# Decode attention beside a gated unit on one core: products with V by two chunks in head-group order, starting three slots later

## The chip, the cores and the metric

The kernel runs on one core of one Trainium2 chip. The metric is the device time of one execution in microseconds (us). For the kernel before, three runs were timed; their median is 198.92 us. One execution was also recorded by the hardware profiler. Engines go by the names of the profile: PE is TensorE (PEld its weight loads), DVE is VectorE, ACT is ScalarE, POOL is GpSimd, SP is SyncE, whose queue (SPq) issues nearly all transfers here.

## What is computed

One decoding step for 8 sequences: attention over the last 2048 entries of a cache, multiplied by a gate from a small feed-forward unit, added to the input. The reference, cut to what matters (B = 8, D = 512, 32 query heads on 8 K/V heads, head size 128, F = 1792; all in bf16):

```
xn = layernorm(x)                                # 8 rows of 512
W  = 2048                                        # the window: the last 2048 of 8192 cache rows
q  = (xn @ wq)                                   # 32 heads of 128 per row
scores = q . k_cache[:, :, -W:, :] * 128 ** -0.5 # 4 query heads share one K/V head
o  = softmax(scores) @ v_cache[:, :, -W:, :]
s  = o @ wo
h  = sigmoid(xn @ w_gate) * (xn @ w_up)
out = x + s * silu(h @ w_down)
```

The windows of K and of V are 33.6 MB each. With the weights, 81.01 MB are read from HBM in one execution.

## The kernel before, in words

**Tiles.** K comes in 8 tiles of 4 MB (four sequences, all 8 heads, a quarter of the window each; line 125), V in 16 tiles of 2 MB (`load_v`, line 137: one sequence, a head group of 4 K/V heads, the whole window in 64 chunks of 32 rows). The sequences fall into two halves, hb = 0 and 1, of four sequences. K tiles 0 to 3 and V tiles 0 to 7 belong to half 0. wq, the K tiles, the gate and up weights, the down weights and wo share a ring of three buffers (KRING); V has a ring of four (VRING). A load can start when the tile three (or four) before it in its ring has been read for the last time.

**Slots.** The order of the work is written out by hand: a loop over slots t (line 651) calls the stages, and each engine runs its instructions in the order in which the loop emits them. Slots 0 to 63 each turn an eighth of a K tile in place on DVE (`k_turn`, line 433, L441). Four slots later `qk` (line 443, L456) multiplies that eighth with the queries on PE; after 8 slots a tile's scores are complete, and a maximum is taken on DVE (L470). EXP_AT is 36 and 68: there `soft_exp` (line 474) makes the exponentials of a half on ACT (L484). One slot later `soft_turn` turns them on DVE (L504), two slots later `soft_spread` spreads them over partitions on PE (L517), copied out by ACT (L525). `soft_mask` (line 531, L539) multiplies them by a mask for each of four heads on DVE, so that one matmul can serve four heads; there is one buffer of these masked exponentials, pT_sb, for both head groups of a half. `soft_den` (line 549) makes the reciprocals of the denominators.

**Products with V.** `pv` (line 580, L595) handles a quarter of a V tile in one slot. PV_AT is 49 for half 0 and 83 for half 1: V tiles 0 to 7 take slots 49 to 80, then two slots are free, and tiles 8 to 15 take slots 83 to 114. The masks are at slots 47 and 48, and at 81 and 82; the denominators at 48 and 82. V tile i is sequence i // 2, head group i % 2. Tiles 0 to 7 are multiplied four chunks at a time (16 matmuls of 128x512 for a tile, two side by side in the array), tiles 8 to 15 two chunks at a time (32 matmuls of 128x256, four side by side). ACT copies the sums out (L606); in the next tile's first slot `pv_sum` (line 609) adds the parts with small f32 matmuls (L616), and DVE scales them (L625).

**Loads.** `issue_loads` (line 198) emits the loads in one fixed order, sorted by the slot of first use (line 184): wq, K0 to K6, V0, V1, K7, V2 to V13, gate and up, V14, V15, down, and wo in eight pieces. All of them are issued by SP in this order, each after a wait for its buffer; a load whose buffer is not free holds back those behind it.

**End.** After the last V tile `o_rows` gathers the heads (L639), `unit_out` makes the gate (L358, with the down weights), and 64 matmuls multiply with wo (L702) as its pieces arrive; two DVE instructions and two small stores end the kernel.

Of the kernel before, what the change touches and what calls it, by code (L numbers as in the profile page):

```python
# [10 lines left out]
def kernel(  # L11
# [13 lines left out]
    nc = tc.nc  # L25
    P = 128
    B, _, D = A_x.shape
    _, Hkv, Sk, Dh = A_k_cache.shape
    Hq = A_wq.shape[1] // Dh
    rep = Hq // Hkv  # L30
# [11 lines left out]
    GL = 4  # L42
    NG = Hkv // GL
    PP = P // GL
    CH = W // PP
    NQ = P // 32
    NJ = 4
    CC = CH // NJ
    NT = B * NG
    NSLOT = NT * NJ  # L50


    HB = B // NQ
# [7 lines left out]
    VSET = NT // HB  # L61
    QK_LAG = 4
    EXP_AT = [SET * (hb + 1) + QK_LAG for hb in range(HB)]
    PV_LAG = 13
    PV_AT = [EXP_AT[0] + PV_LAG]
    for hb in range(1, HB):
        PV_AT.append(max(EXP_AT[hb] + 5, PV_AT[hb - 1] + VSET * NJ + 2))


    NA = Dh // 64  # L70
    CB = CH // 2
    PV_WIDE = VSET
    KRING = 3
    VRING = 4
    NCOL = 2
# [2 lines left out]
    bf16 = mybir.dt.bfloat16  # L78
    f32 = mybir.dt.float32
    AF = mybir.ActivationFunctionType  # L80
    ALU = mybir.AluOpType
    AX = mybir.AxisListType
# [2 lines left out]

    consts = ctx.enter_context(tc.tile_pool(name="consts", bufs=1))
    work = ctx.enter_context(tc.tile_pool(name="work", bufs=1))
    small = ctx.enter_context(tc.tile_pool(name="small", bufs=2))
    kring = ctx.enter_context(tc.tile_pool(name="kring", bufs=KRING))
    vring = ctx.enter_context(tc.tile_pool(name="vring", bufs=VRING))  # L90
# [4 lines left out]
    psum_a = ctx.enter_context(  # L95
        tc.tile_pool(name="psum_a", bufs=3, space=bass.MemoryType.PSUM)
    )
# [25 lines left out]
    v_tiles = {}  # L123

    def load_k(i):
# [8 lines left out]
        )  # L134
        k_tiles[i] = t

    def load_v(i):
        b, gg = divmod(i, NG)
        t = v_tile([P, CH, Dh], "v_sb")
        load(  # L140
            t[:].rearrange("p c d -> p (c d)"),
            A_v_cache[b, GL * gg : GL * (gg + 1), win0:Sk, :].rearrange(
                "j (p c) d -> p j (c d)", c=CH
            ),
        )
        v_tiles[i] = t
# [18 lines left out]
    def load_wo():  # L165
# [19 lines left out]
        (kind, i)  # L185
        for _, kind, i in sorted(
            [(KTS * i, 0, i) for i in range(NKT)]
            + [(NJ * (i % VSET) + PV_AT[i // VSET], 1, i) for i in range(NT)]
        )
    ]  # L190
    loads[-2:-2] = [(2, 0)]
# [6 lines left out]
    def issue_loads():  # L198
# [16 lines left out]
    ident = consts.tile([P, P], bf16, name="ident")  # L215
# [19 lines left out]
        out=rstd[:], in_=mv[:, 1:2], func=AF.Sqrt, bias=eps_t[:], scale=1.0  # L235
# [4 lines left out]
        out=xn_bf[:],  # L240
# [7 lines left out]
    for kt in range(KT):  # L248
        nc.tensor.transpose(
            out=xnT_ps[:, kt, :], in_=xn_bf[:B, kt::KT], identity=ident[:B, :B]  # L250
        )
    x2_ps = psum1.tile([NCOL * 32, DC], f32, name="x2_ps", tag="misc")
    for c in range(NCOL):
        nc.tensor.matmul(
            x2_ps[32 * c : 32 * (c + 1), :],
            lhsT=ident[:B, :32],
            rhs=x_bf[:, DC * c : DC * (c + 1)],
            start=True,
            stop=True,
# [17 lines left out]
        out=PermF[:], in_=ident[:].rearrange("m (h q r) -> m q h r", q=NQ, r=rep)  # L277
# [4 lines left out]
        out=Hm[:],  # L282
        in_=ident[:].rearrange("p (a gl) -> p gl a", gl=GL),
        axis=AX.X,
        op=ALU.add,
# [4 lines left out]
    for j in range(GL):  # L290
        for gg in range(NG):
            g = NG * gg + j // 2
            nc.vector.tensor_copy(
                out=spread[:, gg, j % 2, :, j], in_=ident[:, 32 * g : 32 * g + PP]
            )

    Sel = {}
    for w in (32, 64):
        rows_of = small.tile([P, w], f32, name=f"rows_of{w}")
        nc.vector.tensor_reduce(  # L300
            out=rows_of[:],
            in_=ident[:].rearrange("p (a m) -> p m a", m=w),
            axis=AX.X,
            op=ALU.add,
        )
        Sel[w] = consts.tile([P, w // 16, GL, rep], f32, name=f"Sel{w}")
        by_row = rows_of[:].rearrange("p (h g c r) -> p h c g r", g=GL, c=2, r=rep)
        for c in range(w // 16):
            nc.vector.tensor_copy(out=Sel[w][:, c], in_=by_row[:, c // 2, c % 2])

    NE = P // Hq
    pick = consts.tile([32 * NG, NE, P], bf16, name="pick")
# [1 line left out]
    for gg in range(NG):  # L314
        rows = slice(32 * gg, 32 * (gg + 1))
        cols = slice(NE * GL * rep * gg, NE * GL * rep * (gg + 1))
        for e in range(NE):
            nc.vector.tensor_copy(
                out=pick[rows, e, cols].rearrange("p (h d) -> p h d", d=NE)[:, :, e],
                in_=ident[rows, 32 * gg : 32 * gg + GL * rep],  # L320
# [104 lines left out]
    pT_of = {}  # L425
    den_of = {}
    rden_of = {}
    acc_tiles = {}
# [101 lines left out]

    def soft_mask(hb, gg):

        if gg == 0:
            pT_of[hb] = work.tile(
                [P, NG, NQ * CB, GL, 2 * rep], bf16, name="pT_sb", tag="pT_sb"
            )
        pc = pc_of[hb][:, gg].rearrange("p q (c e) r -> p (q c) (e r)", e=2)
        for gl in range(GL):
            nc.vector.tensor_scalar(  # L539
                out=pT_of[hb][:, gg, :, gl, :],  # L540
                in0=pc,
                scalar1=Hm[:, gl : gl + 1],
                scalar2=None,
                op0=ALU.mult,
            )
# [34 lines left out]
    def pv(t):  # L580


        i, j = divmod(t, NJ)
        b, gg = divmod(i, NG)
        n_ch = 4 if i < PV_WIDE else 2
        w = 16 * n_ch
        if j == 0:
            acc_tiles[i] = psum_a.tile([P, n_ch * Dh], f32, name="acc_ps", tag="acc_ps")
        pT = pT_of[b // NQ][:, gg, CB * (b % NQ) : CB * (b % NQ + 1)].rearrange(
            "p c g n -> p (c g n)"  # L590
        )
        for n in range(CC // n_ch):
            c = n % (P // w)
            ch = CC * j + n_ch * n
            nc.tensor.matmul(  # L595
                acc_tiles[i][w * c : w * (c + 1), :],
                lhsT=pT[:, 16 * ch : 16 * ch + w],
                rhs=v_tiles[i][:, ch : ch + n_ch, :].rearrange("p c d -> p (c d)"),
                start=(j == 0 and n < P // w),
                stop=(j == NJ - 1 and n >= CC // n_ch - P // w),  # L600
                tile_position=(0, w * c),
                skip_group_check=True,
            )
        if j == NJ - 1:
            acc_sb = small.tile([P, n_ch * Dh], f32, name="acc_sb")
            nc.scalar.copy(out=acc_sb[:], in_=acc_tiles.pop(i)[:])  # L606
            acc_sbs[i] = acc_sb

    def pv_sum(i):
        b, gg = divmod(i, NG)  # L610
        n_ch = 4 if i < PV_WIDE else 2
        acc_sb = acc_sbs.pop(i)
        rows = slice(32 * gg, 32 * gg + GW)
        o_ps = psum1.tile([32 * NG, Dh], f32, name="o_ps", tag="misc")
        for c in range(n_ch):
            nc.tensor.matmul(  # L616
                o_ps[rows, :],
                lhsT=Sel[16 * n_ch][:, c].rearrange("p g r -> p (g r)"),
                rhs=acc_sb[:, Dh * c : Dh * (c + 1)],
                start=(c == 0),  # L620
                stop=(c == n_ch - 1),
                tile_position=(0, 32 * gg),
                skip_group_check=True,
            )
        nc.vector.tensor_scalar(  # L625
            out=o_sb[rows, b, :],
            in0=o_ps[rows, :],
            scalar1=rden_of[b // NQ][rows, b % NQ : b % NQ + 1],
            scalar2=None,
            op0=ALU.mult,  # L630
        )
# [16 lines left out]
        )  # L648

    KSLOT = NKT * KTS  # L650
    for t in range(PV_AT[-1] + VSET * NJ):
        u = -1
        for hb, at in enumerate(PV_AT):
            if 0 <= t - at < VSET * NJ:
                u = t - at + VSET * NJ * hb
        if QK_LAG + KTS <= t <= KSLOT + QK_LAG and (t - QK_LAG) % KTS == 0:
            soft_max_part((t - QK_LAG) // KTS - 1)
        for hb in range(HB):
            if t == EXP_AT[hb]:
                soft_exp(hb)  # L660
            for gg in range(NG):
                if t == PV_AT[hb] - NG + gg:
                    soft_mask(hb, gg)
        if t < KSLOT:
            k_turn(t)
        if t == 1:
            q_out(1, q_tiles[1], (0,))
        for hb in range(HB):
            if t == EXP_AT[hb] + 1:
                soft_turn(hb)  # L670
        if QK_LAG <= t < KSLOT + QK_LAG:
            qk(t - QK_LAG)
        if u >= NJ and u % NJ == 0:
            pv_sum(u // NJ - 1)
        if u >= 0:
            pv(u)
        for hb in range(HB):
            if t == EXP_AT[hb] + 2:
                soft_spread(hb)
            if t == PV_AT[hb] - 1:  # L680
                soft_den(hb)
        if t >= QK_LAG and (t - QK_LAG) % KTS == KTS - 1:
            released.add((0, (t - QK_LAG) // KTS))
        if u >= 0 and u % NJ == NJ - 1:
            released.add((1, u // NJ))
        issue_loads()
        if u == NSLOT - 2 * NJ - 1:
            unit_in(wgu_sb[0])
            unit_in(wgu_sb[1])
            released.add((2, 0))  # L690
            issue_loads()
        if u == NSLOT - 2 * NJ:
            unit_mid()
# [6 lines left out]
    for k in range(KW):  # L700
        for c in range(NCOL):
            nc.tensor.matmul(  # L702
                a_ps[32 * c : 32 * (c + 1), :],
                lhsT=o2_sb[:, k, :],
                rhs=wo_parts[k][:, DC * c : DC * (c + 1)],
                start=(k == 0),
                stop=(k == KW - 1),
# [8 lines left out]
    for c in range(NCOL):  # L716
        queues[c].dma_start(
            out=out.flatten_outer_dims()[:, DC * c : DC * (c + 1)],
# [32 lines left out]
```

## Time and profile before

| what | value |
|---|---|
| three timed runs | 197.73, 198.92, 199.18 us; median 198.92 |
| the profiled execution's own time | 199.89 us |
| its span, first to last instruction | 198.1 us |
| DVE busy | 110.8 us (56%), of it 73.9 in the K turns |
| PE busy | 99.1 us (50%); granted clock 0.854 on average |
| ACT busy | 29.1 us (15%) |
| transfers | 81.16 MB, 410 GB/s on average over the span |

The span is 1.8 us shorter than the execution's own time; what lies around it is the launch and the end. The profiled execution took 0.97 us longer than the median of the timed runs, so that a saving read from the trace is subtracted from the median, not from the profiled time. In the timeline of the trace a line gives the start and the duration of an instruction or of a merged group, its engine, line, operation and tile, and in square brackets how long the engine had been idle before it and what released it.

### The profile page before, as it was taken

What the parts mean: (1) busy time and instruction counts of PE and PEld (TensorE: products, weight loads), DVE (VectorE), ACT (ScalarE), POOL (GpSimd) and SP (SyncE); (2) the same over time, 40 slices, a digit from 0 to 9 for tenths busy, and PEclk for the clock granted to TensorE, in tenths of its full rate; (3) what the DMA queues carried; (4) which work ended last, traced back from release to release, by engine and by line L of the source; (5) the groups of instructions that cost most, each with busy time, mean ns of one, the idle gap of its engine ahead of it and who ended that gap; (6) DMA issues with size and microseconds to landing.
All of it is one profiled execution on the core that took longest, in us unless ns stands there. A gap on an engine that the chain in (4) does not pass through costs nothing.

```text
span 198.1 us, 2316 instructions
## 1 busy us (share of the span) xinstructions
PE 99.1 (50%) x950; PEld 43.9 (22%) x950; DVE 110.8 (56%) x182; ACT 29.1 (15%) x69; POOL 1.6 (1%) x8
## 2 busy tenths in 40 slices
PE   0133024434333039314986984888277633545693
PEld 0010001101011012001222331334045421223381
DVE  4706499999899969997995832501711100030301
ACT  3006050000000264000110115151101003000000
POOL 3000000000000000000000000000000000000000
PEclk9999999999999999855897999589958995555569
DMA  7999999999999999899999999999998999999990
GB/s 260 443 443 443 424 419 424 430 424 420 430 463 430 450 443 423 377 440 450 430 417 427 424 443 424 427 409 384 424 430 334 425 426 433 442 427 416 415 377 20
DMA packets 5242, 81.16 MB, mean 410 GB/s; under 512 B 600, under 2 KB 880, under 8 KB 1392
## 3 DMA queue, kind: packets, MB, share of 16 engines
q1 hardware_dynamic: 5200, 81.01, 96.4%
q8 instruction: 7, 0.11, 0.2%
q10 hardware_dynamic: 32, 0.01, 0.0%
q14 instruction: 3, 0.02, 0.0%
HBM read 81.01 MB, written 0.01 MB: 409 GB/s over the span
## 4 chain that ended last, share of the span: by engine, by line
DMA 53%; PE 20%; DVE 18%; ACT 6%; issue 2%; SPq 1%; ACTq 0%; DVEq 0%
DMA k_sb<-in_A_k_cache_dram 20%; DMA wd_sb<-in_B_w_down_dram 15%; DMA v_sb<-in_A_v_cache_dram 13%; DVE k_sb L441 12%; PE acc_ps L595 8%; PE o_ps L616 5%; DMA wo_sb<-in_A_wo_dram 5%; PE s_ps L456 3%; ACT p_bf L484 3%; PE pT_ps L517 2%; ACT acc_sb L606 2%; DVE pT_sb L539 2%; DVE pt_bf L504 1%; DVE mx L470 1%; SPq L108 1%
## 5 line engine op out<-in xcount | busy, mean ns | idle before, releaser
L441 DVE STREAM_TRANSPOSE k_sb<-k_sb 128x1024 f32<-128x1024 f32 x64 | 73.9, 1211 | 4.2 <-DMA k_sb<-in_A_k_cache_dram 4.1
L456 PE MATMUL s_ps<-k_sb,qz_sb 128*32 128x512 bf16 x256 | 29.3, 552 | 47.1 <-DVE k_sb L441 41.3
L595 PE MATMUL acc_ps<-v_sb,pT_sb 128*32 128x256 bf16 (+1 forms) x384 | 34.5, 371 | 9.2 <-DMA v_sb<-in_A_v_cache_dram 9.2
L625 DVE TENSOR_SCALAR o_sb<-o_ps,rden 16x128 bf16<-16x128 f32 x16 | 5.5, 341 | 49.3 <-PE o_ps L616 49.3
L456 PEld LDWEIGHTS <-qz_sb 128*32 128x32 bf16 x256 | 8.4, 114 | 70.7 <-issue 53.6
L616 PE MATMUL o_ps<-acc_sb,Sel 128*16 128x128 f32 x96 | 16.6, 321 | 10.5 <-ACT acc_sb L606 10.2
L606 ACT COPY acc_sb<-acc_ps 128x512 f32<-128x512 f32 (+1 forms) x16 | 7.7, 480 | 77.6 <-PE acc_ps L595 77.6
L595 PEld LDWEIGHTS <-pT_sb 128*32 128x32 bf16 (+1 forms) x384 | 14.4, 112 | 21.1 <-DMA v_sb<-in_A_v_cache_dram 9.0
L616 PEld LDWEIGHTS o_ps<-acc_sb,Sel 128*16 128x16 f32 x96 | 9.3, 109 | 18.0 <-ACT acc_sb L606 15.4
L517 PE MATMUL pT_ps<-pt_bf,spread 128*128 128x512 bf16 x16 | 6.7, 562 | 2.2 <-DVE pt_bf L504 2.0
L504 DVE STREAM_TRANSPOSE pt_bf<-p_bf 128x512 bf16<-128x512 bf16 x8 | 5.0, 680 | 4.8 <-ACT p_bf L484 4.8
L539 DVE TENSOR_SCALAR pT_sb<-pc_bf,Hm 128x1024 bf16<-128x1024 bf16 x16 | 6.5, 475 | 1.6 <-PE acc_ps L595 1.6
L470 DVE TENSOR_REDUCE mx<-s_ps 128x1 f32<-128x512 f32 x8 | 5.3, 667 | 3.6 <-PE s_ps L456 3.6
L382 PE MATMUL q_ps<-wq_sb,xnT_sb 128*32 128x512 bf16 x32 | 3.6, 630 | 7.3 <-DMA wq_sb<-in_A_wq_dram 7.3
L484 ACT ACT_TABLE_LOAD x1 | 1.3, 1283 | 39.7 <-DVE nm L478 39.7
L332 PE MATMUL d_ps<-wgu_sb,xnT_sb 128*32 128x448 bf16 x32 | 3.4, 573 | 5.7 <-DMA wgu_sb<-in_B_w_gate_dram 3.2
L484 ACT ACTIVATE p_bf<-s_ps,nm 128x512 bf16<-128x512 f32 x8 | 5.4, 686 | 4.0 <-DVE nm L478 4.0
L413 ACT COPY qz_sb<-qT_sb 32x32 bf16<-32x32 bf16 x20 | 4.8, 241 | 7.7 <-DVE qT_sb L401 7.5
L525 ACT CAST pc_bf<-pT_ps 128x512 bf16<-128x512 f32 x8 | 4.5, 587 | 8.9 <-PE pT_ps L517 6.3
L702 PE MATMUL a_ps<-wo_sb,o_sb 128*32 128x256 bf16 x64 | 5.2, 312 | 0.1
L568 PE MATMUL den_ps<-ones,dh 128*16 128x1 f32 x32 | 1.4, 166 | 6.9 <-DVE dh L555 6.4
L401 DVE STREAM_TRANSPOSE qT_sb<-q_sb 128x512 bf16<-128x512 bf16 x2 | 1.4, 690 | 6.3 <-ACT q_sb L396 6.3
(59 smaller groups left out, 42.2 us busy)
## 6 DMA issues: line engine op xcount, KB each, us to landing
k_sb<-in_A_k_cache_dram SPq DMA_DIRECT2D x8, 4096.0 KB, 21.9
v_sb<-in_A_v_cache_dram SPq DMA_DIRECT2D x16, 2048.0 KB, 17.9
wq_sb<-in_A_wq_dram SPq DMA_DIRECT2D x1, 4096.0 KB, 12.1
wo_sb<-in_A_wo_dram SPq DMA_DIRECT2D x2, 1024.0 KB
wgu_sb<-in_B_w_gate_dram SPq DMA_DIRECT2D x1, 1792.0 KB
wgu_sb<-in_B_w_up_dram SPq DMA_DIRECT2D x1, 1792.0 KB, 18.3
wd_sb<-in_B_w_down_dram SPq DMA_DIRECT2D x1, 1792.0 KB, 28.9
wo_sb<-in_A_wo_dram SPq DMA_DIRECT2D x3, 512.0 KB, 25.6
```

Of the source, the lines that this page charges most:

```text
L441: nc.vector.transpose(out=kw, in_=kw)
L456: nc.tensor.matmul(s_tiles[i][32 * g : 32 * (g + 1), :], lhsT=qz_sb[:, hb, h, 2 * a + e, :], rhs=kT[:, :, a, h, :, e], start=(n == 0), sto ...
L470: nc.vector.reduce_max(out=mx_of[hb][:, kq : kq + 1], in_=s_tiles[i][:], axis=AX.X)
L484: nc.scalar.activation(out=p_bf[:, :, kq], in_=s_tiles.pop(NK * hb + kq)[:].rearrange("p (o c j) -> p c j o", o=2, j=NC), func=AF.Exp, bia ...
L504: nc.vector.transpose(out=pt[:, w * n : w * (n + 1)], in_=p_bf[:, w * n : w * (n + 1)])
L517: nc.tensor.matmul(pT_ps[:], lhsT=spread[:, gg, y].rearrange("p k g -> p (k g)"), rhs=pt[:, c, y, :], start=(y == 0), stop=(y == 1), skip_ ...
L539: nc.vector.tensor_scalar(out=pT_of[hb][:, gg, :, gl, :], in0=pc, scalar1=Hm[:, gl : gl + 1], scalar2=None, op0=ALU.mult,)
L595: nc.tensor.matmul(acc_tiles[i][w * c : w * (c + 1), :], lhsT=pT[:, 16 * ch : 16 * ch + w], rhs=v_tiles[i][:, ch : ch + n_ch, :].rearrange ...
L606: nc.scalar.copy(out=acc_sb[:], in_=acc_tiles.pop(i)[:])
L616: nc.tensor.matmul(o_ps[rows, :], lhsT=Sel[16 * n_ch][:, c].rearrange("p g r -> p (g r)"), rhs=acc_sb[:, Dh * c : Dh * (c + 1)], start=(c ...
L625: nc.vector.tensor_scalar(out=o_sb[rows, b, :], in0=o_ps[rows, :], scalar1=rden_of[b // NQ][rows, b % NQ : b % NQ + 1], scalar2=None, op0= ...
L702: nc.tensor.matmul(a_ps[32 * c : 32 * (c + 1), :], lhsT=o2_sb[:, k, :], rhs=wo_parts[k][:, DC * c : DC * (c + 1)], start=(k == 0), stop=(k ...
```

## The change: order of V, chunk size, start slot, buffers and places of the softmax stages

1. V tiles are ordered by head group inside a half: tile i of a half is head group i // 4, sequence i % 4 (before, head group i % 2, sequence i // 2). The load order of tile numbers stays as it was.
2. All V tiles are multiplied by two chunks (before, tiles 0 to 7 by four). One selection matrix Sel is left of two.
3. V starts at slot 52 and runs without a gap to slot 115 (before, 49 to 80 and 83 to 114).
4. pT_sb becomes one buffer per half and head group, from a pool of two; each is half as large as the single one before.
5. The turn of the exponentials comes 3 slots after the exponentials (before 1), the spread 4 slots after (before 2), the denominators 5 slots after (before at slots 48 and 82, now 41 and 73). The masks are at slots 45 and 46 for half 0, and at 74 and 84 for half 1.

```diff
-    PV_LAG = 13
-    PV_AT = [EXP_AT[0] + PV_LAG]
-    for hb in range(1, HB):
-        PV_AT.append(max(EXP_AT[hb] + 5, PV_AT[hb - 1] + VSET * NJ + 2))
+    TURN_LAG = 3
+    SPREAD_LAG = 4
+    V_LAG = 49
+    PV_LAG = 52
+    MASK_AT = {}
+    for gg in range(NG):
+        MASK_AT[0, gg] = EXP_AT[0] + 9 + gg
+        MASK_AT[1, gg] = max(EXP_AT[1] + 6, PV_LAG + NJ * NQ * (gg + 1))
...
-    PV_WIDE = VSET
+    NCH = 2
...
+    work2 = ctx.enter_context(tc.tile_pool(name="work2", bufs=2))
...
+    def v_of(i):
+        hb, n = divmod(i, VSET)
+        gg, q = divmod(n, NQ)
+        return NQ * hb + q, gg
+
     def load_v(i):
-        b, gg = divmod(i, NG)
+        b, gg = v_of(i)
...
-            + [(NJ * (i % VSET) + PV_AT[i // VSET], 1, i) for i in range(NT)]
+            + [(NJ * i + V_LAG, 1, i) for i in range(NT)]
...
-        if gg == 0:
-            pT_of[hb] = work.tile(
-                [P, NG, NQ * CB, GL, 2 * rep], bf16, name="pT_sb", tag="pT_sb"
-            )
+        pT_of[hb, gg] = work2.tile([P, NQ * CB, GL, 2 * rep], bf16, name="pT_sb")
...
-        b, gg = divmod(i, NG)
-        n_ch = 4 if i < PV_WIDE else 2
-        w = 16 * n_ch
+        b, gg = v_of(i)
+        w = GL * rep * NCH
...
-    for t in range(PV_AT[-1] + VSET * NJ):
-        u = -1
-        for hb, at in enumerate(PV_AT):
-            if 0 <= t - at < VSET * NJ:
-                u = t - at + VSET * NJ * hb
+    for t in range(PV_LAG + NSLOT):
+        u = t - PV_LAG
...
-                if t == PV_AT[hb] - NG + gg:
+                if t == MASK_AT[hb, gg]:
                     soft_mask(hb, gg)
...
-            if t == EXP_AT[hb] + 1:
+            if t == EXP_AT[hb] + TURN_LAG:
                 soft_turn(hb)
...
-            if t == EXP_AT[hb] + 2:
+            if t == EXP_AT[hb] + SPREAD_LAG:
                 soft_spread(hb)
-            if t == PV_AT[hb] - 1:
+            if t == EXP_AT[hb] + 5:
                 soft_den(hb)
```

More of the change, by code (lines that the diff above doesn't have):

```diff
@@ L295 @@
             )
[L297 to L304, printed above, removed]
-        )
[L306 to L309, printed above, removed]
+    w = NCH * GL * rep
+    rows_of = small.tile([P, w], f32, name="rows_of")
+    nc.vector.tensor_reduce(
+        out=rows_of[:],
+        in_=ident[:].rearrange("p (a m) -> p m a", m=w),
+        axis=AX.X,
+        op=ALU.add,
+    )
+    Sel = consts.tile([P, NCH, GL, rep], f32, name="Sel")
+    nc.vector.tensor_copy(
+        out=Sel[:], in_=rows_of[:].rearrange("p (g c r) -> p c g r", g=GL, c=NCH)
+    )
     NE = P // Hq
@@ L531, in soft_mask @@
     def soft_mask(hb, gg):
-        if gg == 0:
-            pT_of[hb] = work.tile(
-                [P, NG, NQ * CB, GL, 2 * rep], bf16, name="pT_sb", tag="pT_sb"
-            )
+        pT_of[hb, gg] = work2.tile([P, NQ * CB, GL, 2 * rep], bf16, name="pT_sb")
         pc = pc_of[hb][:, gg].rearrange("p q (c e) r -> p (q c) (e r)", e=2)
@@ L539, in soft_mask @@
             nc.vector.tensor_scalar(
-                out=pT_of[hb][:, gg, :, gl, :],
+                out=pT_of[hb, gg][:, :, gl, :],
                 in0=pc,
@@ L583, in pv @@
         i, j = divmod(t, NJ)
-        b, gg = divmod(i, NG)
-        n_ch = 4 if i < PV_WIDE else 2
-        w = 16 * n_ch
+        b, gg = v_of(i)
+        w = GL * rep * NCH
         if j == 0:
[L588 to L592, printed above, removed]
+            acc_tiles[i] = psum_a.tile([P, NCH * Dh], f32, name="acc_ps", tag="acc_ps")
+        q = b % NQ
+        pT = pT_of[b // NQ, gg][:, CB * q : CB * (q + 1)].rearrange("p c g n -> p (c g n)")
+        for n in range(CC // NCH):
             c = n % (P // w)
-            ch = CC * j + n_ch * n
+            ch = CC * j + NCH * n
             nc.tensor.matmul(
                 acc_tiles[i][w * c : w * (c + 1), :],
-                lhsT=pT[:, 16 * ch : 16 * ch + w],
-                rhs=v_tiles[i][:, ch : ch + n_ch, :].rearrange("p c d -> p (c d)"),
+                lhsT=pT[:, GL * rep * ch : GL * rep * ch + w],
+                rhs=v_tiles[i][:, ch : ch + NCH, :].rearrange("p c d -> p (c d)"),
                 start=(j == 0 and n < P // w),
-                stop=(j == NJ - 1 and n >= CC // n_ch - P // w),
+                stop=(j == NJ - 1 and n >= CC // NCH - P // w),
                 tile_position=(0, w * c),
@@ L604, in pv @@
         if j == NJ - 1:
-            acc_sb = small.tile([P, n_ch * Dh], f32, name="acc_sb")
+            acc_sb = small.tile([P, NCH * Dh], f32, name="acc_sb")
             nc.scalar.copy(out=acc_sb[:], in_=acc_tiles.pop(i)[:])
@@ L609, in pv_sum @@
     def pv_sum(i):
-        b, gg = divmod(i, NG)
-        n_ch = 4 if i < PV_WIDE else 2
+        b, gg = v_of(i)
         acc_sb = acc_sbs.pop(i)
@@ L614, in pv_sum @@
         o_ps = psum1.tile([32 * NG, Dh], f32, name="o_ps", tag="misc")
-        for c in range(n_ch):
+        for c in range(NCH):
             nc.tensor.matmul(
                 o_ps[rows, :],
-                lhsT=Sel[16 * n_ch][:, c].rearrange("p g r -> p (g r)"),
+                lhsT=Sel[:, c].rearrange("p g r -> p (g r)"),
                 rhs=acc_sb[:, Dh * c : Dh * (c + 1)],
                 start=(c == 0),
-                stop=(c == n_ch - 1),
+                stop=(c == NCH - 1),
                 tile_position=(0, 32 * gg),
```

## The prediction

> **What bounds the kernel now.** I read the page's slices first, then the chain, then windows by stage, then the timeline of SP's issues and of PE. Slices and chain:
>
> ```profile
> DMA  7999999999999999899999999999998999999990
> GB/s 260 443 443 443 424 419 424 430 424 420 430 463 430 450 443 423 377 440 450 430 417 427 424 443 424 427 409 384 424 430 334 425 426 433 442 427 416 415 377 20
> ...
> q1 hardware_dynamic: 5200, 81.01, 96.4%
> ...
> DMA 53%; PE 20%; DVE 18%; ACT 6%; issue 2%; SPq 1%; ACTq 0%; DVEq 0%
> ```
>
> The transfers are the bound: 16 engines busy for 96.4% of the span, no compute engine above 56%. The bytes stay the same, so a gain can only come from slices in which the transfers ran below their rate; slices 27 (384) and 30 (334) stand out in the second half. The windows (engines' busy time, PE clock, DMA share, GB/s) enclose them:
>
> ```profile
> 20.00:60.00 40.00, 13.28 (x112) 4.14 (x113) 36.78 (x38) 2.90 (x12) 0.00 (x0) 1.00 1.00 432
> ...
> 110.00:132.00 22.00, 17.11 (x118) 6.45 (x116) 9.21 (x15) 6.59 (x15) 0.00 (x0) 0.84 1.01 430
> 132.00:141.00 9.00, 6.03 (x52) 3.03 (x48) 2.13 (x6) 1.76 (x3) 0.00 (x0) 1.00 0.95 381
> 141.00:148.00 7.00, 4.12 (x56) 2.72 (x56) 2.86 (x10) 0.00 (x0) 0.00 (x0) 0.69 1.01 433
> 148.00:160.00 12.00, 7.77 (x149) 5.12 (x148) 1.70 (x5) 1.86 (x5) 0.00 (x0) 0.90 0.97 393
> 160.00:184.00 24.00, 11.13 (x140) 5.75 (x141) 2.34 (x5) 2.94 (x5) 0.00 (x0) 0.59 1.00 427
> ```
>
> Two troughs, 132 to 141 and 148 to 160, each beside a stretch at 430 to 433. SP's issues show why:
>
> ```profile
> 120.97 0.54 SPq L108 DMA_DIRECT2D v_sb<-in_A_v_cache_dram  x1
> 132.27 0.54 SPq L108 DMA_DIRECT2D v_sb<-in_A_v_cache_dram  x1
> 135.85 0.54 SPq L108 DMA_DIRECT2D v_sb<-in_A_v_cache_dram  x1
> 139.48 0.54 SPq L108 DMA_DIRECT2D v_sb<-in_A_v_cache_dram  x1
> 148.22 0.53 SPq L108 DMA_DIRECT2D v_sb<-in_A_v_cache_dram  x1
> ```
>
> These are V8 to V12. A V tile (2.10 MB) takes 4.9 us at 432 GB/s, and V2 landed at 106.3 (PE waits for it until then), so V7 lands near 130.7 and V8 near 135.6: when V9 is issued at 132.27, V8 alone is in flight. The queue refills until 139.48, then 8.7 us pass without an issue. A load waits for the tile four before it to be read, so the products are late. The timeline names the two delays:
>
> ```profile
> 106.31 1.07 PE L595 MATMUL acc_ps<-v_sb,pT_sb 128*64 128x512 bf16 x4 [1.69 <-DMA v_sb<-in_A_v_cache_dram]
> 123.92 2.49 DVE L504 STREAM_TRANSPOSE pt_bf<-p_bf 128x512 bf16<-128x512 bf16 x4 [2.86 <-ACT p_bf L484]
> 137.52 1.92 PE L595 MATMUL acc_ps<-v_sb,pT_sb 128*64 128x512 bf16 x16
> 139.56 3.26 DVE L539 TENSOR_SCALAR pT_sb<-pc_bf,Hm 128x1024 bf16<-128x1024 bf16 x8 [1.58 <-PE acc_ps L595]
> 157.26 1.06 PE L595 MATMUL acc_ps<-v_sb,pT_sb 128*32 128x256 bf16 x32 [1.01 <-DMA v_sb<-in_A_v_cache_dram]
> 180.44 1.90 PE L595 MATMUL acc_ps<-v_sb,pT_sb 128*32 128x256 bf16 x32 [1.45 <-DMA v_sb<-in_A_v_cache_dram]
> ```
>
> Half 1's softmax (120 to 131) lies between products; then its masks wait for the last product of half 0, which still reads the one buffer, and with the denominators they cost 139.5 to 144.6 before the next product. From 157.26 on PE waits for V again.
>
> **The change part by part.**
>
> *Chunks.* A wide tile takes 16 matmuls in 1.92 us, a narrow one 32 in 1.06, both at a granted clock of 1.00 (1.90 at a low clock, 180.44). For eight tiles PE gains 8 x 0.86 = 6.9 us. The copy falls from 0.59 to 0.37 us, the small f32 matmuls from 8 in 1.05 to 4 in 0.61. None of this is on the path while transfers bind: it only brings releases forward, by up to 1.5 us a tile.
>
> *Selection matrices.* One reduction and five copies fewer on DVE, some 0.8 of the 1.3 us between 6.8 and 8.1; DVE then idles 6.3 us for the queries. Zero.
>
> *Turn and spread of half 0, two slots later.* DVE idled 1.94 us at 72.4 for the exponentials; two more K turns (2 x 1.16) fill it. The spread still starts with the turn's end. Denominators at slot 41 put 8 + 8 tiny matmuls (0.35 + 0.37 us) and their DVE round trip behind the spread on PE: up to 1.5 us of DVE waiting near 78, against about 1 us that leaves slot 48. K4's last product, which frees K7's buffer, may come 0.6 us later than 79.5; K6, V0 and V1 are queued then until about 92. Cover 12 us, so zero; without the cover it would be 0.6.
>
> *V three slots later.* V0's first product stood behind DVE's denominators until 92.94. In slot 52 it needs K turn 48; with masks (2 x 1.63) and maxima in between I count that turn's end at about 91.6. V4's issue, which waits for V0's last product (K turn 51), comes near 96 instead of 97.54. K7, V2 and V3 are queued until 111, so three slots (3.5 us) cost nothing even if this count is off.
>
> *Half 1.* V2 and V3 are still read on landing (106.3 and 111.2), now in slots 60 to 67, in which K7's scores end too. So exponentials start near 113.5 and not at 121.1. V4 lands at 116, and its four slots 68 to 71 need nothing of half 1. The turn (2.5) ends near 119.5; the spread is emitted behind V5's first products (V5 lands 120.9) and takes 3.1 us (128.09 to 131.2 now); V5 is read by about 125.5. Then V9 is issued near 125.5 (132.27 now), V10 near 127.5 (135.85), V11 near 132 (139.48).
>
> *Masks and buffers.* Head group 0 of half 1 is masked in slot 74, near 125 to 127, in a buffer last read by V3; V8 needs it at 135.6. Head group 1 waits at slot 84 for V7's last product (read near 132) and takes 1.63 us; queued behind it on DVE is only the scaling of V7's result, whose readers wait for nothing near. V12 needs that mask near 155. So the stall of 139.5 to 144.6 goes, and V12's issue moves from 148.2 to near 137. What is late next is V's landing itself, every 4.9 us.
>
> *Transfers.* Count, size and order stay. With two to three tiles always queued, both troughs fill at the rate of 20 to 60 us: 9.00 x (1 - 381/432) = 1.06 and 12.00 x (1 - 393/432) = 1.08, together 2.15 us. A second way: V2 to V12 is ten tiles in 157.26 - 106.31 = 50.95 us, against 10 x 4.9 = 49.0 (2.0 less) or, at 432 GB/s to the byte, 48.5 (2.4 less). I take 2.15 and keep 1.6 and 2.6 as ends. SP issues the same instructions, and POOL is not touched.
>
> [...]
>
> *The end.* Down, wo and the last products are chained to V15's landing (180.44) and move with it. One cost is unknown, PE's clock: 28 of 32 matmuls of L358 take 3.17 us at the end and L702 5.30 for 64, at a mean clock of 0.73. From 32 products in 1.06 and 1.90 us, a clock that stayed low would stretch these 8.5 us by at most about a tenth, 0.8 us, part of it still under wo's landing; a higher clock gains nothing, since wo's last piece lands at 194.6, 0.3 us before the last matmul starts to end. I take 0, the case that the trace shows, and keep +0.8.
>
> Sum against the profiled execution: 199.89 - 2.15 = 197.74. The median of the timed runs is 198.92, so 198.92 - 2.15 = 196.77: I predict 196.8, 1.1% less.
>
> **The rivals.**
>
> *Only one trough goes.* If the spread of half 1 holds PE so long that V9's issue slips past 130.7, where V8 alone is in flight, the first trough stays and only the one after the masks (1.08) fills: 197.8. For it: the spread still sits between V5's products. Against: 5 us of margin.
>
> *The troughs are not hunger.* If the rate dips there for another cause, as in slice 16 (377, with more than 10 us queued), nothing changes: 198.9. Against: 433 in 141 to 148, between the two, with V10 and V11 queued.
>
> *The end takes it back.* A low clock throughout the end gives 196.8 + 0.8 = 197.6. [...]
>
> *Slower: the new order of V lowers the rate.* Consecutive V tiles were the two head halves of one sequence; now they come from different sequences. If HBM served that worse, 33.6 MB of V (77.7 us at 432) would pay: a fall of 2.8% eats the gain, and one of 5.5% (408) costs 4.3 us and ends at 201.1. It decides from there on. Against: a K tile spans four sequences in one load and moves at 432 as well.
>
> **How the numbers follow.** Both troughs filled: 0.66, with its own range 196.3 to 197.5 (2.6 gained, to 1.6 gained with little of the end's cost). One trough or the end's cost: 0.17. No hunger: 0.08. Slower order: 0.09. About 1% is what a measurement of this kernel can tell from no change, so the border is 196.93; three quarters of the first case lie beyond it. Faster by over 1%: 0.50. Within 1%: 0.16 + 0.17 + 0.08 = 0.41. Slower: 0.09. The range 195.8 to 198.6 holds the first two cases, with the spread of the three timed runs (1.45 us) on the lower side, and leaves out the slower order and most of no hunger, some 0.17.
>
> **What would show it.** Right: windows after 110 us at 427 to 433 without a trough; V9's issue near 125, V12's near 137; masks of half 1 without 139.5's stall; V15's landing near 178; the last matmuls 2 us earlier. Wrong: a window under 400 with two V tiles queued (no hunger), an issue gap above 7 us after 120 (a new wait), V tiles more than 5.0 us apart with the queue full (the order), or a longer way from V15's landing to the end than the 14.5 us of now (the clock).

## The result and the profile after

| | before | changed |
|---|---|---|
| executions timed together | 22 | 22 |
| median | 199.25 us | 197.93 us |
| lowest to highest | 197.73 to 201.13 | 197.65 to 198.33 |
| profiled execution | 199.89 (span 198.1) | 198.09 (span 196.3) |

The ratio of changed to before is 0.9946, with a 95% interval of 0.9923 to 0.9968: a gain of 0.54%, half of the 1.1% forecast. (It leaves out executions over 1.5% above the fastest of the same kernel, so that it lies nearer to 1 than the medians' ratio.) Two things are to be explained: why the gain is half of the forecast, and why the kernel before spreads over 3.4 us and the changed one over 0.7.

The profiled execution itself went nearly as forecast. The page of the changed kernel, slices, rate and chain:

```profile
DMA  6999999999999999999999999999999999999990
GB/s 235 447 441 434 441 429 441 427 434 424 434 427 427 427 427 434 417 424 451 441 414 431 427 427 427 429 431 431 427 431 427 434 430 435 424 426 423 422 363 19
...
DMA 59%; DVE 27%; PE 9%; issue 1%; SPq 1%; ACT 0%; ACTq 0%; DVEq 0%
```

Its windows, with the columns of the prediction's windows:

```profile
110.00:132.00 22.00, 14.35 (x230) 7.81 (x222) 9.58 (x22) 6.78 (x17) 0.00 (x0) 0.84 1.01 431
132.00:141.00 9.00, 3.08 (x52) 1.75 (x52) 2.35 (x6) 0.74 (x2) 0.00 (x0) 0.80 1.00 426
141.00:148.00 7.00, 4.55 (x69) 2.38 (x62) 0.34 (x1) 0.74 (x2) 0.00 (x0) 0.50 1.02 438
148.00:160.00 12.00, 6.86 (x76) 3.40 (x76) 1.02 (x3) 0.74 (x2) 0.00 (x0) 0.50 1.00 426
```

Both troughs are gone: 426 where 381 and 393 stood. PE's clock was no better: 0.84 from 110 to 132 as before, and 0.50 from 141 to 160. The products merely had more time in hand. SP's issues of V9 to V12, and the lines of DVE and PE around half 1's softmax:

```profile
127.63 0.54 SPq L113 DMA_DIRECT2D v_sb<-in_A_v_cache_dram  x1
129.60 0.54 SPq L113 DMA_DIRECT2D v_sb<-in_A_v_cache_dram  x1
132.11 0.54 SPq L113 DMA_DIRECT2D v_sb<-in_A_v_cache_dram  x1
136.96 0.54 SPq L113 DMA_DIRECT2D v_sb<-in_A_v_cache_dram  x1
...
126.36 0.17 DVE L583 RECIPROCAL rden<-den_ps 16x4 f32<-16x4 f32 x1 [4.93 <-PE den_ps L574]
...
127.20 1.68 DVE L545 TENSOR_SCALAR pT_sb<-pc_bf,Hm 128x1024 bf16<-128x1024 bf16 x4
132.19 1.67 DVE L545 TENSOR_SCALAR pT_sb<-pc_bf,Hm 128x1024 bf16<-128x1024 bf16 x4 [1.11 <-PE acc_ps L599]
...
135.85 1.06 PE L599 MATMUL acc_ps<-v_sb,pT_sb 128*32 128x256 bf16 x32 [2.65 <-DMA v_sb<-in_A_v_cache_dram]
```

From V8 (135.85) on the first products of every tile wait for V's landing and for nothing else (eight waits, at most 2.6 us). V15 lands at 178.37 (forecast: near 178; before: 180.44).

### The profile page after: what moved, and what is told of

Read it like the earlier page. It is cut to its first block, busy times and chain, and to the rows that moved or that the text cites. A ratio compares the mean times of both kernels' runs of the same rounds, so it can differ in the third digit from the quotient of the medians.

```text
span 196.3 us, 2503 instructions
## 1 busy us (share of the span) xinstructions
PE 90.5 (46%) x1046; PEld 43.9 (22%) x1046; DVE 109.9 (56%) x176; ACT 27.4 (14%) x69; POOL 1.6 (1%) x8
## 4 chain that ended last, share of the span: by engine, by line
DMA 59%; DVE 27%; PE 9%; issue 1%; SPq 1%; ACT 0%; ACTq 0%; DVEq 0%
DVE k_sb L450 22%; DMA k_sb<-in_A_k_cache_dram 20%; DMA v_sb<-in_A_v_cache_dram 15%; DMA wgu_sb<-in_B_w_up_dram 13%; DMA wo_sb<-in_A_wo_dram 12%; PE pT_ps L526 3%; PE acc_ps L599 3%; PE s_ps L465 2%; DVE pT_sb L545 2%; DVE mx L479 1%; DVE pt_bf L513 1%; PE a_ps L702 1%; SPq L113 1%; PE den_ps L574 1%; PE o_ps L619 0%
## 5 line engine op out<-in xcount | busy, mean ns | idle before, releaser
L465 PE MATMUL s_ps<-k_sb,qz_sb 128*32 128x512 bf16 x256 | 33.3, 585 | 56.5 <-DVE k_sb L450 50.7
L599 PE MATMUL acc_ps<-v_sb,pT_sb 128*32 128x256 bf16 x512 | 31.4, 367 | 17.4 <-DMA v_sb<-in_A_v_cache_dram 17.4
L465 PEld LDWEIGHTS <-qz_sb 128*32 128x32 bf16 x256 | 10.3, 121 | 73.8 <-issue 53.2
L599 PEld LDWEIGHTS <-pT_sb 128*32 128x32 bf16 x512 | 17.9, 121 | 28.9 <-DMA v_sb<-in_A_v_cache_dram 21.3
L610 ACT COPY acc_sb<-acc_ps 128x256 f32<-128x256 f32 x16 | 6.0, 373 | 81.1 <-PE acc_ps L599 81.1
L619 PE MATMUL o_ps<-acc_sb,Sel 128*16 128x128 f32 x64 | 14.1, 362 | 6.9 <-ACT acc_sb L610 6.9
L619 PEld LDWEIGHTS o_ps<-acc_sb,Sel 128*16 128x16 f32 x64 | 6.6, 118 | 13.9 <-ACT acc_sb L610 11.5
L526 PE MATMUL pT_ps<-pt_bf,spread 128*128 128x512 bf16 x16 | 7.5, 622 | 0.9 <-DVE pt_bf L513 0.7
L702 PE MATMUL a_ps<-wo_sb,o_sb 128*32 128x256 bf16 x64 | 5.7, 324 | 0.9 <-DMA wo_sb<-in_A_wo_dram 0.8
L702 PEld LDWEIGHTS <-o_sb 128*32 128x32 bf16 x64 | 4.4, 117 | 2.3 <-issue 1.9
```

The lines of the kernel that those rows point to most:

```text
L465: nc.tensor.matmul(s_tiles[i][32 * g : 32 * (g + 1), :], lhsT=qz_sb[:, hb, h, 2 * a + e, :], rhs=kT[:, :, a, h, :, e], start=(n == 0), sto ...
L526: nc.tensor.matmul(pT_ps[:], lhsT=spread[:, gg, y].rearrange("p k g -> p (k g)"), rhs=pt[:, c, y, :], start=(y == 0), stop=(y == 1), skip_ ...
L599: nc.tensor.matmul(acc_tiles[i][w * c : w * (c + 1), :], lhsT=pT[:, GL * rep * ch : GL * rep * ch + w], rhs=v_tiles[i][:, ch : ch + NCH, : ...
L619: nc.tensor.matmul(o_ps[rows, :], lhsT=Sel[:, c].rearrange("p g r -> p (g r)"), rhs=acc_sb[:, Dh * c : Dh * (c + 1)], start=(c == 0), stop ...
L702: nc.tensor.matmul(a_ps[32 * c : 32 * (c + 1), :], lhsT=o2_sb[:, k, :], rhs=wo_parts[k][:, DC * c : DC * (c + 1)], start=(k == 0), stop=(k ...
```

## The experiments

**The theories.** A: the gain is troughs refilled. They come when V's products are late by more than the queue holds, which in the kernel before depends on the execution, through PE's granted clock; whatever issues V9 to V12 some us earlier removes them, and below that lies a floor near 197.7. B: the spread has another cause (HBM, the end of the kernel). C: the single buffer of masked exponentials is the cause. D: only the narrow products matter. Of each kernel, 9 to 12 executions were timed beside the kernel before; "spread" is highest less lowest.

### The kernel before again

No edit.

> The kernel before, unchanged, to see its own spread: 22 timed executions of it ran from 197.73 to 201.13 us, those of the changed kernel from 197.65 to 198.33. Theory A (hunger that depends on PE's clock): the size of the two troughs differs from one execution to the next, because PE's products between V2 and V12 run at a granted clock that differs; executions with a low mean clock take 199.5 to 201, those with a high one 197.7 to 198.3, and the profile taken here shows troughs that fit its time. Theory B (the spread comes from HBM or from the end): times spread alike, without a relation to the clock or to the troughs; a fast execution shows the same two troughs of 1 us each.

Measured: median 198.96, 197.50 to 201.73; ratio 0.9982 (0.9939 to 1.0025). The profiled execution took 197.70, less than the changed kernel's median:

```profile
110.00:132.00 22.00, 16.13 (x128) 6.94 (x128) 8.15 (x15) 6.81 (x16) 0.00 (x0) 1.00 1.00 428
132.00:141.00 9.00, 3.90 (x44) 2.08 (x40) 4.30 (x13) 1.17 (x2) 0.00 (x0) 0.85 1.01 431
141.00:148.00 7.00, 5.84 (x103) 4.03 (x107) 0.82 (x3) 0.74 (x2) 0.00 (x0) 0.71 1.00 426
148.00:160.00 12.00, 5.85 (x94) 3.29 (x85) 1.22 (x4) 1.12 (x3) 0.00 (x0) 0.81 1.01 428
```

The same kernel, and no trough. V9 is issued at 128.73 here and at 132.27 in the execution of the prediction, V12 at 144.70 and 148.22. The granted clock is the difference. Here it is 1.00 from 97.3 to 138.3. The execution of the prediction has 0.50 in two stretches of that time, one over V2's products and one in half 1's softmax (a third, behind the masks, has its like here from 138.3 to 145.1):

```profile
106.14:109.56 3.42, 3.25 (x18) 0.75 (x19) 1.29 (x3) 0.00 (x0) 0.00 (x0) 0.50 1.00 426
123.20:130.00 6.80, 5.55 (x20) 2.15 (x21) 2.76 (x5) 1.63 (x5) 0.00 (x0) 0.50 1.01 431
143.70:150.50 6.80, 5.73 (x81) 3.75 (x82) 0.98 (x4) 0.37 (x1) 0.00 (x0) 0.50 0.91 371
```

PE's lines, first in the execution of the prediction, then here:

```profile
124.42 1.89 PE L616 MATMUL o_ps<-acc_sb,Sel 128*16 128x128 f32 x8 [3.49 <-ACT acc_sb L606]
126.24 1.92 PE L595 MATMUL acc_ps<-v_sb,pT_sb 128*64 128x512 bf16 x8
```

```profile
106.28 0.62 PE L595 MATMUL acc_ps<-v_sb,pT_sb 128*64 128x512 bf16 x4 [0.99 <-DMA v_sb<-in_A_v_cache_dram]
123.01 1.05 PE L616 MATMUL o_ps<-acc_sb,Sel 128*16 128x128 f32 x8 [3.49 <-ACT acc_sb L606]
123.99 1.05 PE L595 MATMUL acc_ps<-v_sb,pT_sb 128*64 128x512 bf16 x8
```

V2's first products start together (106.31 and 106.28) but take 1.07 us there and 0.62 here; by L616 the lag is 1.41 us. The second stretch, in which V5's eight products ahead of the spread take 1.92 us there and 1.05 here, adds 2.13, and that makes the 3.54 us of V9's issue. The masks (139.56 against 136.01) and V12's issue only carry them on. PE idles for the same 3.49 us ahead of L616 in both, and only in one does the clock fall. Over the 135 executions of the kernel before that were recorded in these series there are two families. In one (67) the mean clock is near 0.70. The profiled execution with each narrow product twice, whose mean is as low (0.688), has 0.50 from 20 to 60 us, where PE waits for DVE anyway (the execution of the prediction has 1.00 there, and PE busy for 13.28 of 40 us). This low stretch probably hides the rest in the mean: the mean clock tells little of the time (correlation -0.22). In the other (68) time and mean clock go together (-0.77): at most 0.857, the median time is 200.4 (24 executions); above it, 198.1 (44). That is A, not B; but a correlation is no test, which the idle matmuls below are.

### Only the later start

```diff
-    PV_LAG = 13
+    PV_LAG = 16
```

> The kernel before with V started three slots later and nothing else (slots 52 to 83 and 86 to 117; masks and denominators go with it). Theory A, the start slot does it: K7's scores end before PE waits for V4, half 1's exponentials come near 114 and not 121, V9 is issued before 129, and what the masks of half 1 cost (about 5 us after V7) is hidden, since V8 lands only near 135.6; both troughs go, and the time is 197.9, like the changed kernel, with as little spread. Theory C, the masks' single buffer does it: the first trough shrinks, the second stays, and the time is 198.7.

Measured: median 198.67, 197.70 to 201.91; ratio 0.9989 (0.9951 to 1.0026). A missed the time. C's number came out, but not its reason: the profiled execution (198.42) has no trough (425 to 433 GB/s in the four windows from 110 to 160), and the spread stayed, at 4.2 us. V9 was issued at 129.06 and V12 at 145.03, no earlier than in the execution of the kernel before at 197.70 (128.73 and 144.70), so the later start alone gives no margin. The start slot alone is worth nothing measurable.

### Only the narrow products

```diff
-    PV_WIDE = VSET
+    PV_WIDE = 0
```

> The kernel before with all products by two chunks and nothing else. Theory A: each of tiles 0 to 7 is read 0.9 us sooner at most, but half 1's exponentials still stand behind V4's arrival (116) and come near 119, and the masks still wait for V7; V9 is issued near 130, V12 near 143. Half of the hunger stays: 198.5. Theory D (the narrow products are the whole gain, by freeing PE): 197.9 and little spread.

Measured: 197.71, 197.50 to 197.91; ratio 0.9942 (0.9910 to 0.9974). One constant gives the whole gain. V9 is issued at 127.15 and V12 at 139.81, 5 us before the execution at 197.70 above. My estimate for A was too small (V12 near 143), and D stands so far.

### The change with wide products

```diff
+    PV_WIDE = VSET
...
+        n_ch = 4 if i < PV_WIDE else 2
```

> The changed kernel with tiles 0 to 7 multiplied by four chunks again; order, buffers, start slot and places of the softmax stay. Theory A (margin: the troughs come when half-clock windows of PE delay the products by more than the queue holds, and any part that issues V9 to V12 some 4 us earlier cures it): exponentials still come near 114, no stall after V7; 197.9 with a spread under 1 us. Theory D (only the narrow products matter, the rest of the change is idle): 199.2 with a spread of 3 us, like before.

Measured: 197.70, 197.58 to 197.90; ratio 0.9950 (0.9922 to 0.9978). D falls: without the narrow products the rest of the change gives the same gain and the same small spread. Either is enough, and together they give no more.

### The change with one buffer

```diff
-        MASK_AT[1, gg] = max(EXP_AT[1] + 6, PV_LAG + NJ * NQ * (gg + 1))
+        MASK_AT[1, gg] = PV_LAG + VSET * NJ
...
-        pT_of[hb, gg] = work2.tile([P, NQ * CB, GL, 2 * rep], bf16, name="pT_sb")
+        if gg == 0:
+            both = work.tile([P, NG, NQ * CB, GL, 2 * rep], bf16, name="pT_sb", tag="pT_sb")
+            for g2 in range(NG):
+                pT_of[hb, g2] = both[:, g2]
```

> The changed kernel with one buffer for both head groups of the masked exponentials again, so that half 1's masks wait for V7's last product (slot 84). Theory A: the stall returns (3.3 us of masks after V7, near 132 to 136), but V8 lands only near 135.6 and V9 to V11 have been issued by then; 197.9, spread under 1 us. Theory C (the single buffer is a cause by itself): a trough near 145 to 155, 198.5 or more.

Measured: 197.88, 197.43 to 197.96; ratio 0.9941 (0.9910 to 0.9972). As A expected: the masks may wait for V7, since V8 has not landed. C falls as a cause by itself.

### Only order and buffers

```diff
-        b, gg = divmod(i, NG)
+        b, gg = v_of(i)
...
-                if t == PV_AT[hb] - NG + gg:
+                if t == ((47, 48), (74, 81))[hb][gg]:
```

(with one buffer per half and head group, as in the change)

> The kernel before with the order by head group and two buffers (half 1's masks at slots 74 and 81), wide products, start and softmax places as before. Theory A: the stall after V7 goes (V12 near 143 in an execution like the one profiled first), so the second trough goes; the first depends on V5's products behind half 1's softmax and stays in executions with half-clock windows near 125: median 198.5, a spread of about 2 us. Theory D: 199.2, as before.

Measured: median 198.01, 197.64 to 200.12; ratio 0.9995 (0.9954 to 1.0036). Six of twelve executions lie at or below 197.80, as in the cured versions, six from 198.23 to 200.12. Part of the margin, as A had it; a gain is not shown. Two buffers alone have no run: in the old order each holds both head groups, and V's ring, 64.47 KB per partition, doesn't fit beside them (57.19 KB are left).

### Half tiles of V

```diff
-    VRING = 4
+    VRING = 8
...
-        if u >= 0 and u % NJ == NJ - 1:
-            released.add((1, u // NJ))
+        if u >= 0 and u % 2 == 1:
+            released.add((1, u // 2))
```

(and `load_v` and the load order by halves of the window's chunks)

> The kernel before with V in tiles of 1 MB and a ring of eight (the same 8 MB of buffer): a load can start as soon as half a V tile has been read. No instruction of PE, DVE or ACT changes. Theory A (hunger): loads are issued some 1 to 2 us earlier in the stretch after 120, the troughs shrink: median 198.4 and fewer executions above 200. Theory B (the spread has another cause than late issues): 199.2 with the same spread, or more if packets of half the size are slower.

Measured: 198.43, eleven of twelve from 198.27 to 198.64, one 199.59; ratio 0.9979 (0.9945 to 1.0012). Without a change to any compute instruction the spread is gone: late issues are what it consists of, and this speaks against B. The level is 0.7 us above the floor; the rate with half tiles is lower (422 GB/s from 92 to 106 and 428 from 120 to 132, against 431 and 434 in the execution of the prediction).

### Idle matmuls in PE's waits

```diff
+        if t == EXP_AT[1] + 1:
+            warm(12)
+        if t == PV_AT[1] - 2:
+            warm(12)
```

> The kernel before with two bursts of twelve idle matmuls (128x512, into a PSUM tile that nothing reads) where PE waits in half 1: in slot 69, while ACT makes the exponentials, and in slot 81, while DVE masks. They add about 3 us of PE work each (5 at half clock) inside waits of 4.0 and 4.3 us. Theory A with the clock as the cause of the spread: the half-clock windows after these waits (123 to 130 and 144 to 150 in the execution profiled first) do not come; median 198.0, few executions above 199. Theory E (it is PE's work that counts and not its clock): the bursts can only hinder; median 199.2 or more, the same spread.

Measured: 197.75, 197.57 to 198.30; ratio 0.9934 (0.9908 to 0.9960). More work on PE, nothing taken away, and the whole gain. The idle burst, and the clock behind it:

```profile
120.72 2.76 PE L612 MATMUL w_ps<-spread,ident 128*128 128x512 bf16 x12
```

```profile
121.00:131.00 10.00, 7.93 (x48) 3.39 (x47) 2.71 (x5) 5.96 (x14) 0.00 (x0) 1.00 1.01 430
131.00:143.50 12.50, 9.93 (x105) 5.37 (x103) 4.70 (x15) 1.17 (x2) 0.00 (x0) 1.00 1.01 430
```

V9 is issued at 129.98 instead of 132.27, V12 at 144.95 instead of 148.22. Up to the burst this execution runs like that of the prediction (V4's last eight products begin at 119.73 and 119.88). This is the test of the clock as the cause, and E falls. In the kernel before, the half-clock stretches between 100 and 155 us last 3.4 or 6.8 us and begin at other times in other executions (138.3 in the one at 197.70, where the masks make PE wait anyway: it is busy for 4.31 of 6.80 us). In the traces of the kernel before and of the changed kernel every entry of the clock, from 78.8 and 79.4 us on, is 1.00 or 0.50, and every stretch but the last lasts a whole multiple of 3.41 us, from 3.41 to 44.4. What starts a stretch at 0.50 is not shown: the wait of 3.49 us ahead of L616 comes with one in one execution and not in the other.

### Each narrow product twice

```diff
+            if i < VSET:
+                nc.tensor.matmul(
+                    acc_tiles[i][w * c : w * (c + 1), 2 * Dh :],
...
```

(on narrow products alone)

> The kernel before with narrow products only, where each product of V tiles 0 to 7 is done twice, the second time into columns that nothing reads: PE's products of a tile cost 2.1 us at full clock, as much as the wide ones (1.9), while the copies and the small f32 matmuls stay as short as in the run with narrow products alone. Theory A: the margin that the narrow products gave is gone; median 198.9, a spread of 2 us or more. Theory F (the gain of the narrow products lies in the shorter copies and f32 matmuls, or in the array's tile shape, which no longer changes between the products with K and V): 197.7 and a spread of 0.4 us, as with narrow products alone.

Measured: 198.87, 198.68 to 199.14; ratio 0.9995 (0.9969 to 1.0021). The median is A's number and the spread is F's, and A's reason is wrong: no trough in the slices (422 to 439 GB/s from 110 to 180 us). V's landings equal those of narrow products alone up to the up weights (168.46); V14 and V15 land 1.15 us later. The trace has ten transfers of instructions (queue q8, 16 KB each) instead of eight.

### Idle matmuls early, where PE is free

```diff
+        if 12 <= t < 28:
+            idle(16)
```

(on narrow products alone)

> Narrow products alone, with 256 idle matmuls of 128x32 (sixteen in each of slots 12 to 27, in the K stage, where PE is idle two thirds of the time; nothing reads what they write). The run with each product done twice took 1.2 us more than narrow products alone without a trough: its trace has 10 transfers of instructions (16 KB each) instead of 8, the bytes moved by 180 us are the same, and two 16 KB packets of V15 end at 178.5 and 179.1 where the others end by 177.9. Theory G (the 1.2 us is the ninth and tenth transfer of instructions, which come round to DMA engines that had one already, and a tile lands with its last engine): 10 such transfers here too, V14 or V15 landing about 1 us late, 198.8 with little spread. Theory H (it is PE's work on V): 197.7, as with narrow products alone.

Measured: 198.83, 198.71 to 199.15; ratio 0.9993 (0.9969 to 1.0017), as G expected. Transfers of instructions in the page's third part (packets, MB, share), narrow products alone and then with the early idle matmuls:

```profile
q8 instruction: 8, 0.13, 0.2%
```

```profile
q8 instruction: 10, 0.16, 0.3%
```

PE's first products of V15 in the timeline, in the same order:

```profile
178.36 1.90 PE L595 MATMUL acc_ps<-v_sb,pT_sb 128*32 128x256 bf16 x32 [1.38 <-DMA v_sb<-in_A_v_cache_dram]
```

```profile
179.35 1.90 PE L595 MATMUL acc_ps<-v_sb,pT_sb 128*32 128x256 bf16 x32 [1.39 <-DMA v_sb<-in_A_v_cache_dram]
```

Two 16 KB packets of V15 end at 178.31 and 178.92, all others by 177.8. The tenth transfer starts only at 189.37, after V15, so G's reason can hold for the ninth alone (167.77). So 256 matmuls that no one waits for cost 1.1 us, over a hundred us later.

### Copies and sums twice

```diff
+            if i < VSET:
+                nc.scalar.copy(out=acc_sb[:], in_=acc_tiles[i][:])
...
-        for c in range(n_ch):
+        for c in list(range(n_ch)) * (2 if i < VSET else 1):
```

(on narrow products alone)

> Narrow products alone, but for V tiles 0 to 7 ACT copies the sums twice and the f32 matmuls of L616 are done twice (the second start clears the first), so that the copy and the sums cost what they cost with wide products (0.74 against 0.59 us; 8 matmuls). Theory A with the products as the source of the margin: 197.8 and a spread under 1 us. Theory F (the margin of the narrow version lies in the shorter copies and sums): 199.0 and a spread of 2 us, like before.

Measured: 197.71, 197.62 to 198.24; ratio 0.9929 (0.9906 to 0.9953). The shorter copies and sums are not needed.

### Products, copies and sums twice

Both edits above together.

> Narrow products with products, copies and sums of V tiles 0 to 7 all done twice, so that each of the three costs at least what it costs with wide products (2.1 against 1.9 us, 0.74 against 0.59, 8 matmuls). By the run with idle matmuls its floor lies at 198.8, because it has ten transfers of instructions or more. Theory A (the narrow version's margin is the sum of shorter products and shorter copies and sums; either half was enough): the margin is gone, half of the executions have troughs; median 199.6, a spread of 2 us or more. Theory F' (the margin lies in something that neither of them is: the array's shape, which stays the same between the products with K and V, or a stream that keeps the clock up): 198.9 and a spread under 0.6 us.

Measured: median 199.00, 198.72 to 200.00; ratio 1.0005 (0.9980 to 1.0031). Above the floor of 198.8 the median is 0.2 higher, and four of twelve exceed 199.4; the profiled execution (199.02) has the second trough again:

```profile
148.00:160.00 12.00, 6.64 (x142) 4.37 (x134) 1.71 (x5) 1.49 (x4) 0.00 (x0) 0.91 0.99 404
```

So a part of the narrow version's margin is its shorter products, copies and sums, of which either half is enough. By these numbers it is the smaller part: the 22 executions of before have their median 1.5 above their floor of 197.7, against 0.2 here, so A's 199.6 was too high and F' came nearer in the median, though not in the spread (1.28, four of twelve astray). What the rest is stays open: the array's shape, the denser stream's clock, or a higher floor that hides a part of a trough.

## Why the prediction was wrong on the gain and right on the steps

**Right: the bound, the place and the mechanism.** Transfers bound the kernel; the troughs were hunger; the steps of half 1 came in the order laid out, the first two about 2 us late: V9 was issued at 127.63 (125.5 forecast), V10 at 129.60 (127.5), V11 at 132.11 (132), V12 at 136.96 (137), and V15 landed at 178.37 (178). From 132 to 160 us the windows add up to 11.18 MB before (9 x 381 + 7 x 433 + 12 x 393) and 12.01 MB after: 0.84 MB more, 1.94 us at 432 GB/s, against 2.15 forecast. The two profiled executions differ by 1.80 us. The split into two equal troughs does not hold, though. By the trace before, a tile's last part came 7.31 us after that of the tile ahead at V9, and 4.84 to 4.87 after it at V10, V11 and V12: with 4.85 for a full queue, all 2.46 us were lost in the first trough. In the second, the parts that had run ahead waited (V11's parts landed from 149.24 to 152.35, V12's from 155.14 to 157.22), so by these landings filling it alone would have gained nothing, where the rival of one trough counts 1.08.

**Wrong: "The median of the timed runs is 198.92, so 198.92 - 2.15".** The step took the troughs of one execution, the profiled one at 199.89, off the median of others. It treated the 0.97 us between them as an offset that stays, as the text ahead of the prediction does. It does not stay: the troughs are a part of that difference. A floor near 197.7 is reached by the kernel before in its best executions (197.50) and, within 0.3 us, by the cured versions with seven or eight transfers of instructions and full tiles; what a cure takes away is each execution's own distance from it. For the profiled one that is 2.2, for the median of the 22 timed together 1.5, for the three runs shown at the time 0.0, 1.2 and 1.5. So of 198.92 no more than 1.2 us could go, and not 2.15. The sum against the profiled execution's own time, 197.74, is 0.2 from the measured median of 197.93: that number should have been the forecast, with the three runs' lowest, 197.73, as a sign of the floor.

**Half seen: the clock.** I priced it at the kernel's end and as V's products at 1.06 or 1.90, but took the half-clock stretches in the middle for the kernel's own pace. Those at 106.1 and 123.2 are not in the execution at 197.70, and they are what pushed V9 and V12 out by 3.5 us.

**Parts.** That three slots later cost nothing held; alone they also gave nothing. "None of this is on the path" for the narrow products was wrong for the kernel before: alone they give the whole gain, just because they bring releases forward. V4 was issued at 98.43, not near 96. The exponentials began at 115.26, not 113.5. Not foreseen: denominators in slot 73 queue on PE behind the spread, DVE waits 4.93 us for them, and the first masks come at 127.20; they end 7 us before V8 lands, which covered it.

**Rivals.** One trough only, no hunger and a slower order did not come; V tiles land 4.85 us apart in the new order. The end took nothing: from V15's landing to the store's issue it is 15.31 us, 15.29 before.

## What to carry to other kernels

A stall seen in one profiled execution is that execution's; before it is subtracted, it must be asked whether the timed runs have it, and their lowest is a bound on what its removal alone can give. Where a queue runs dry because a chain of short waits lies under a clock that falls in some executions (here to 0.50 where another has 1.00), margin ahead of the late issues is enough, wherever it comes from (the later start alone gave none), and a burst of idle matmuls shows cheaply that the clock is the cause. The best versions here (197.70 to 197.75: narrow products alone, the change with wide products, or idle matmuls in the kernel before) are not told apart from each other, and none lies clearly below the whole change.

## What the runs showed of the hardware

With ten transfers of instructions (queue q8, 16 KB each) instead of eight, each narrow product twice and the early idle matmuls took 1.16 and 1.12 us more than narrow products alone (198.87 and 198.83 against 197.71), far from the instructions that were added. The kernel before with idle matmuls in PE's waits has seven and took 197.75. The durations of these transfers repeat with a period of eight (962, 964, 948, 879, 879, 935, 929, 924, then 962 and 960 ns in the run with products twice), so I read them as going round eight of the engines that carry the data. The ninth (168.55 there) then gave one engine its second before V15 landed; the tenth (189.41) came after. This is inferred, since the trace does not name the engine. The cost was not hidden in these two runs, in which the packets of the data (q1) take 96.3% of the 16 engines' span.

PE's first product of V15 started just after the last of that tile's sixteen parts had landed. With the early idle matmuls fifteen parts are in by 178.11, the last one comes at 179.31, and the product starts at 179.35. In the changed kernel the parts land from 176.21 to 178.32, and the product starts at 178.37.
